# HGRN2 attention and a gelu MLP on one core: the decay's sigmoid through Tanh and GpSimd, and turned keys read in place by TensorE

## The chip, the cores and the metric

The kernel runs on one core of a Trainium2 chip. The core has a matrix engine (TensorE, PE in the profile, with its weight loads on a row of their own, PEld), VectorE (DVE), ScalarE (ACT), GpSimd (POOL) and a DMA issuer (SyncE, SP). The engines work side by side and wait for each other through semaphores. The metric is the device time of the launch in microseconds.

## The reference, cut to what matters

```python
# B, H, S, D = 4, 8, 768, 48; all float32
f = 1.0 / (1.0 + np.exp(-f_logit))
for t in range(S):
    state = f[:, :, t, :, None] * state + np.einsum('bhd,bhe->bhde', k[:, :, t], v[:, :, t])
    y[:, :, t] = np.einsum('bhd,bhde->bhe', q[:, :, t], state)
x = y.transpose(0, 2, 1, 3).reshape(3072, 384)
h = x @ w_in                                  # 384 -> 2048
g = h * (1.0 / (1.0 + np.exp(-1.702 * h)))
out = g @ w_out                               # 2048 -> 384
```

## The kernel before

The 3072 tokens are worked in 12 **units** of 256 tokens, n = 0 to 11, three for each of the four batches. Inside a unit the recurrence is not stepped token by token. The decays F = sigmoid(f_logit) are multiplied together in a tree of six levels (block lengths 1, 2, 4 to 32); at each level the keys and queries in X are scaled by the products (`promote`) and TensorE makes a product of keys and queries (`score`), so that a chunk of 64 tokens becomes a masked 64 by 64 matrix A. What a chunk hands on is a state of 48 by 48 for each head, made from turned keys (tokens on the partitions) and values. Each unit is held as two halves of 128 tokens, f = 1 in time order and f = 0 backwards, and as two heads (h) of four pairs (a).

After attention, a unit's 256 rows of y are brought into xT and go through the MLP: h = xT by `w_in` (line 785), g by one ScalarE instruction straight out of PSUM (line 789, `Gelu_apprx_sigmoid`), and the product with `w_out` (line 811 for the first three units, line 762 for the rest).

The lines that the change and the prediction touch:

- `begin_f`, line 358, through `turn`, line 326: brings the unit's f_logit into F, tokens along the free axis. Units 0 to 2 are turned by TensorE (line 344) and written out of PSUM by four ScalarE instructions (line 349), which apply the sigmoid on the way in units 0 and 1; unit 2 copies first and applies it in one instruction on the whole of F (line 355). Units 3 to 11 are turned by two VectorE transposes (line 332), and one ScalarE instruction over 128 x 1024 applies the sigmoid in place (line 337).
- `begin_gates`, line 377: six GpSimd multiplies (line 383) that make the tree of products `tot` from F. They are in one queue with whatever else GpSimd is given. Level 0 of `promote` reads F itself (line 473 in units 0 to 2, line 477 after).
- The turned keys `kn`. Units outside `CARRY` turn them on TensorE (line 532) and copy them out with ScalarE (line 533). The seven units in `CARRY`, n = 4 to 10, send them through memory instead: VectorE transposes blocks into z (line 540), four DMAs write them to a DRAM tile and one reads them back as kt, tokens on the partitions (line 554). In kt the four pairs of a column lie side by side: the innermost index is a. ScalarE copies kt to `kn`, where the columns of one pair are contiguous (line 555).
- Part "S", line 568: 64 matmuls (line 576), one for each pair, half, head and 64-token group, each with a 64 by 64 weight load from `kn`. They lie in turn on four quarters of the array (group g sets the rows, head h the columns). The states (lines 591 to 595, VectorE) are made from their result.

The order of the work on TensorE is written out by hand all through (`manual_schedule`): `merge` puts the matmuls of earlier units' MLP between the parts of a unit's attention. For the first four units the emission order holds on every engine (`fill_order`); from unit 4 on, the order on the other engines is a planner's. PSUM gives the products and turns four buffers in common (tag "mm"). kt and z take turns in three SBUF buffers (tag "sum"), `kn` and yT share one (tag "kn").

ScalarE's functions come from tables, and the sigmoid and the g of line 789 are in different ones: the compiler puts an ACT_TABLE_LOAD ahead of each change.

Of the kernel before, what the change touches and what calls it, by code (L numbers as in the profile page):

```python
# [9 lines left out]
F32 = mybir.dt.float32  # L10
I32 = mybir.dt.int32
U32 = mybir.dt.uint32
AF = mybir.ActivationFunctionType
ALU = mybir.AluOpType


def view(t, offset, dims):

    a = t[:]
    return bass.AP(a.tensor, a.offset + offset, [list(a.ap[0])] + [list(d) for d in dims])  # L20
# [3 lines left out]
def kernel(  # L24
# [33 lines left out]
    nc = tc.nc  # L58
# [3 lines left out]
    P = 128  # L62
# [6 lines left out]
    NP = H // 2  # L69
    HS = 64  # L70
# [6 lines left out]
    N_FILL = 3  # L77
    HALF = U // 2
    SLOT = NP * HALF
    NA = NP * U  # L80
    NALL = B * NU
    CARRY = range(N_FILL + 1, NALL - 1)
# [6 lines left out]
    mlp = ctx.enter_context(tc.tile_pool(name="mlp", bufs=2))  # L89
# [58 lines left out]
    F = const.tile([P, NA], F32, name="F")  # L148
# [21 lines left out]
    for r in range(NGR):  # L170
        ffs = range(r * FG, (r + 1) * FG)
        for ff in ffs[::2]:
            f = slice(ff * P, (ff + 2) * P)
# [65 lines left out]
    def load_raw(n, j, engines=(nc.sync,)):  # L239
        if n >= NALL:  # L240
            return
        b, s0 = n // NU, n % NU * U
        src = (f_logit, q, k)[j]
        first = s0 - (j == 1)

        def span(head, token, dims, d=0):
            return bass.AP(src.tensor, src.offset + ((b * H + head) * S + token) * D + d, dims)
        if n < N_FILL:
            for a in range(NP):
                engine = engines[a * len(engines) // NP]  # L250
                to = by_pair[j][32 * a:32 * (a + 1), :, :R * D]
                if first < 0 and a == 0:

                    for r, rows in ((1, 16), (17, 15)):
                        engine.dma_start(
                            out=to[r:r + rows], in_=span(0, r * R - 1, [[R * D, rows], [S * D, 2], [1, R * D]])
                        )
                    engine.dma_start(out=to[:1, :, D:], in_=span(0, 0, [[R * D, 1], [S * D, 2], [1, (R - 1) * D]]))
                else:
                    engine.dma_start(out=to, in_=span(2 * a, first, [[R * D, 32], [S * D, 2], [1, R * D]]))  # L260
            return
        for f in (1, 0):
            for r in range(4):
                lo = 32 * (r % 2)
                width = R4 * D - lo
                part = span(r // 2, first + (0 if f else HALF), [[R4 * D, 32], [2 * S * D, NP], [1, width]], lo)
                nc.sync.dma_start(out=by_half[32 * r:32 * (r + 1), j, f, :, :width], in_=part)
            if f and first < 0:
                for r in range(4):
                    lo = 32 * (r % 2)  # L270
                    nc.sync.dma_start(
                        out=by_half[32 * r:32 * r + 1, j, f, :, :D - lo],
                        in_=q[b - 1, r // 2::2, S - 1:S, lo:].rearrange("a t d -> t a d"),
                    )
# [31 lines left out]
    def attention(n):  # L306
# [8 lines left out]
        ORDER = (1, 0) if n % 2 == 0 else (0, 1)  # L315
        R_BASE, L_BASE = max(KR, QF) - 1, max(KF, QR) - 1
        t = {"tms": [F]}
        parts = []

        def part(kind):  # L320
            return lambda fn: parts.append((kind, fn))
# [4 lines left out]
        def turn(j, outs, fn=None):  # L326

            if n >= N_FILL:
                for f in (1, 0):
                    out = outs(f)  # L330
                    at, step = (0, 1) if f else (HALF - 1, -1)
                    nc.vector.transpose(  # L332
                        view(out, at, [[HALF, NP], [step, R4], [R4 * step, 32]]),
                        by_half[:, j, f].rearrange("p a (j d) -> p (a j) d", j=R4)[:, :, :32],
                    )
                if fn:
                    nc.scalar.activation(F, F, fn)
                return
            for j0 in range(0, R, 4):
                pt = ps.tile([P, 4, P], F32, tag="mm", name=f"t_{n}_{j}_{j0}", bufs=4)  # L340
                for jj in range(4):
                    for h in range(2):
                        x = (j0 + jj) * D
                        nc.tensor.matmul(  # L344
                            pt[h * HS:(h + 1) * HS, jj, :], lhsT=by_pair[j][:, h, x:x + HS], rhs=ident, start=True, stop=True
                        )
                for f in (1, 0):
                    at, step = (j0, 1) if f else (HALF - 1 - j0, -1)
                    nc.scalar.activation(
                        view(outs(f), at, [[HALF, NP], [R * step, 16], [step, 4]]),  # L350
                        pt.rearrange("p j (a f i) -> p f a i j", a=NP, f=2)[:, 1 - f],
                        fn if fn and n < N_FILL - 1 else AF.Copy,
                    )
            if fn and n == N_FILL - 1:
                nc.scalar.activation(F, F, fn)

        def begin_f():
            turn(0, lambda f: F[:, ORDER.index(f) * SLOT:(ORDER.index(f) + 1) * SLOT], AF.Sigmoid)
            if n >= N_FILL or (n == 1 and 0 == 0):
                load_raw(n + 1, 0)  # L360

        def begin():
            turn(1, lambda f: slot(query(n, f)))
            if n >= N_FILL or (n == 1 and 1 == 0):
                load_raw(n + 1, 1)
# [45 lines left out]
        def scores():  # L411
            t["sc"] = ps.tile([P, 2, NP, 2, HS], F32, tag="sc", name=f"sc_{n}_{next(serial)}")
            return t["sc"]
# [67 lines left out]
        def add():  # L481


            t["py"] = ps.tile([P, NG, NP, 2, HS], F32, tag="y", name=f"y_{n}")
            for a in range(NP):
                for f in (1, 0):
                    for h, g in TILES:
                        nc.tensor.matmul(  # L488
                            t["py"][columns(h, g), g, a, f, :],
                            lhsT=vts[n][g * HS:(g + 1) * HS, f, (2 * a + h) * D:(2 * a + h + 1) * D],  # L490
                            rhs=A[g * HS:(g + 1) * HS, h * NP + a, f, :],
                            start=(f == 1 and a == 0), stop=False, skip_group_check=True,
                        )
# [28 lines left out]
        def new_kn():  # L522
            t["kn"] = att.tile([P, NP, 2, P], F32, tag="kn", name=f"kn_{n}", bufs=1)
# [24 lines left out]
                )  # L548

        def fetch_k(f):  # L550
            if f == 0:
                new_kn()
            z = mlp.tile([P, P, NP], F32, tag="sum", name=f"kt_{n}_{f}", bufs=3)
            nc.sync.dma_start(out=z.rearrange("p d a -> p (d a)"), in_=k_toks[n % 2][f].rearrange("t i x -> t (i x)"))
            nc.scalar.copy(t["kn"][:, :, f, :], z.rearrange("p d a -> p a d"))

        if n not in CARRY:
            for a0 in (0, 2):
# [8 lines left out]
        @part("S")  # L567
        def _():
            add()
            pd = scores().rearrange("p h a s t -> p h (a s t)")  # L570
            for a in range(NP):
                for f in (1, 0):
                    for h in range(2):
                        for g in range(NG):
                            x = (a * 2 + f) * D
                            nc.tensor.matmul(  # L576
                                pd[h * HS:(h + 1) * HS, g, x:x + D],
                                lhsT=t["kn"][g * HS:(g + 1) * HS, a, f, h * HS:(h + 1) * HS],
                                rhs=vts[n][g * HS:(g + 1) * HS, f, (2 * a + h) * D:(2 * a + h + 1) * D],
                                start=True, stop=True,  # L580
                            )
            load_v(n + 1)
            st = att.tile([P, NC, NP, D], F32, tag="st", name=f"st_{n}", bufs=2)
            D64 = t["tms"][NL].rearrange("p (f a g) -> p f g a", f=2, a=NP)
            prev = t["ahead"] = last.get("st")
            t["before"] = [prev[:, NC - 1] if c == 0 and not first else st[:, c - 1] if c else None for c in range(NC)]
            for c in range(NC):
                g, f = CHUNK[c]
                d = pd[:, g, :NP * 2 * D].rearrange("p (a f e) -> p f a e", a=NP, f=2)[:, f]
                if t["before"][c] is None:  # L590
                    nc.vector.tensor_copy(st[:, c], d)
                    continue
                by = D64[:, ORDER.index(f), g].unsqueeze(2).broadcast_to((P, NP, D))
                nc.vector.tensor_tensor(st[:, c], t["before"][c], by, ALU.mult)  # L594
                nc.vector.tensor_tensor(st[:, c], st[:, c], d, ALU.add)
            last["st"] = st
# [418 lines left out]
```

## Time and profile before

Three runs took 628.22, 628.49 and 629.21 us, median 628.49; the profiled execution spans 627.9 us. The page gives a row to each engine; a busy time is a union, so overlapping matmuls are counted once.

| | us | count |
|---|---|---|
| span of the profiled execution | 627.9 | |
| DVE busy | 385.8 | 632 |
| ACT busy | 260.3 | 544 |
| of it: g, 128 x 256 and 128 x 257 | 72.1 | 192 |
| of it: table loads, 1.283 us each | 25.7 | 20 |
| of it: kt copied to kn, 128 x 512 | 15.9 | 14 |
| of it: sigmoid on the whole of F (lines 337, 355) | 10.6 | 10 |
| POOL busy | 39.9 | 91 |
| PE: the matmuls of part S, line 576 | 13.6 | 768 |

In the listing of instructions in order of time, a row gives the start, the length, the engine, the line, the operation with output and inputs, the number of instructions merged in the row, and in brackets how long the engine had stood idle before it and on whom it waited. "p*q" ahead of a matmul's shape is the rows and columns of the array that it uses.

### The profile page before, as it was taken

To read this page: it belongs to the slowest core of one execution; us is meant where nothing else is said; L and a number is where in the kernel's file an instruction comes from. 1 tells how busy PE (TensorE), PEld (TensorE's weight loads), DVE (VectorE), ACT (ScalarE), POOL (GpSimd) and SP (SyncE) were. 2 spreads that over 40 slices of the span, in tenths; PEclk is the share of its full clock that TensorE was granted. 3 is DMA by queue.
4 is the path that set the end of the run, shared out by engine and by line. 5 is a ranking of instruction groups with operands and counts; after the bars stand their busy time and mean duration, and the time that the engine had idled before them with its cause. 6 is when DMAs were issued, how large, how long until landed. Compare 5 with 4: busy or idle time off the path is not lost.

```text
span 627.9 us, 17094 instructions
## 1 busy us (share of the span) xinstructions
PE 602.8 (96%) x7314; PEld 517.5 (82%) x7314; DVE 385.8 (61%) x632; ACT 260.3 (41%) x544; POOL 39.9 (6%) x91
## 2 busy tenths in 40 slices
PE   7958999889999999999999999999999999999997
PEld 5647776757678688989989989989989889889896
DVE  1778976575876755677566577656658645521441
ACT  3436543533244534543544454354354353233220
POOL 3010030020001001001001001001001001000000
PEclk9898999989999999999999999999999999999999
DMA  7646675652034444444452342552161121001000
GB/s 171 183 126 165 170 161 158 148 139 76 2 92 99 122 100 105 105 94 110 122 135 60 76 109 73 142 123 68 45 160 33 44 59 27 27 1 27 26 1 25
DMA packets 83308, 58.20 MB, mean 93 GB/s; under 512 B 33633, under 2 KB 75265, under 8 KB 83233
## 3 DMA queue, kind: packets, MB, share of 16 engines
q1 hardware_dynamic: 82192, 55.55, 35.4%
q10 hardware_dynamic: 1041, 1.57, 1.0%
q8 instruction: 57, 0.93, 0.7%
q14 instruction: 18, 0.15, 0.1%
HBM read 43.98 MB, written 8.39 MB: 83 GB/s over the span
## 4 chain that ended last, share of the span: by engine, by line
PE 87%; DVE 6%; ACT 3%; DMA 2%; issue 1%; SPq 1%; ACTq 0%; DVEq 0%
PE h L785 38%; PE o_X L762 8%; PE o_Y L762 8%; PE o L811 8%; PE o_Z L762 7%; PE sc L392 6%; PE o_W L762 4%; PE t L344 3%; PE y L616 2%; PE sc L576 2%; PE y L488 1%; PE idle L108 1%; DVE a L221 1%; DMA xT<-yT 1%; ACT yT L627 1%
## 5 line engine op out<-in xcount | busy, mean ns | idle before, releaser
L785 PE MATMUL h<-xT,w_in 128*128 128x256 f32 (+1 forms) x1152 | 257.4, 381 | 2.4 <-ACT g L789 1.9
L785 PEld LDWEIGHTS h<-xT,w_in 128*128 128x128 f32 x1152 | 216.4, 190 | 34.2 <-ACT g L789 2.1
L789 ACT ACTIVATE g<-h 128x256 f32<-128x256 f32 (+1 forms) x192 | 72.0, 383 | 156.8 <-PE h L785 156.5
L477 DVE TENSOR_TENSOR X<-X,tot 128x1024 f32<-128x1024 f32 x45 | 55.1, 1224 | 62.6 <-PE sc L392 49.4
L448 ACT COPY Kc<-X 128x512 f32<-128x512 f32 x72 | 48.0, 666 | 83.4 <-DVE X L477 51.3
L811 PE MATMUL o<-w_out,g 128*128 128x384 f32 x192 | 67.5, 501 | 3.0 <-DVE w_out L222 3.0
L811 PEld LDWEIGHTS o<-w_out,g 128*128 128x128 f32 x192 | 36.2, 194 | 26.0 <-DVE w_out L222 3.6
L762 PE MATMUL o_X<-w_out,g 128*128 128x192 f32 x288 | 52.6, 331 | 0.0
L762 PE MATMUL o_Y<-T,S 128*128 128x192 f32 x288 | 51.9, 329 | 0.0
L441 DVE COPY_PREDICATED A<-masks,sc 128x256 f32<-128x256 uint32 (+1 forms) x108 | 50.9, 534 | 0.1
L762 PEld LDWEIGHTS o_Y<-T,S 128*128 128x128 f32 x288 | 46.9, 190 | 1.5 <-issue 0.7
L762 PEld LDWEIGHTS o_X<-w_out,g 128*128 128x128 f32 x288 | 46.7, 190 | 1.0
L383 POOL TENSOR_TENSOR tot<-F 128x512 f32<-128x512 f32 x12 | 12.5, 1039 | 478.2 <-DVE st L594 429.3
L392 PE MATMUL sc<-X,Kc 48*64 48x64 f32 x1440 | 31.1, 224 | 10.7 <-ACT Kc L448 9.6
L392 PEld LDWEIGHTS sc<-X,Kc 48*64 48x64 f32 x1440 | 26.4, 138 | 18.0 <-ACT Kc L448 11.4
L332 DVE STREAM_TRANSPOSE X<-raw 128x512 f32<-128x512 f32 x36 | 37.9, 1101 | 2.9 <-PE y L616 2.8
L700 DVE TENSOR_TENSOR g<-g,g 128x512 f32<-128x512 f32 x18 | 12.5, 692 | 40.4 <-ACT g L789 40.4
L627 ACT COPY yT<-y 48x256 f32<-48x256 f32 x92 | 33.7, 366 | 7.8 <-PE y L616 5.3
L473 DVE TENSOR_TENSOR X<-X,tot 128x512 f32<-128x512 f32 x30 | 20.3, 688 | 13.1 <-PE sc L392 11.0
L383 POOL TENSOR_TENSOR tot<-tot 128x256 f32<-128x256 f32 (+4 forms) x60 | 24.6, 410 | 4.7
L762 PE MATMUL o_W<-T,g 128*128 128x192 f32 x144 | 24.9, 326 | 0.0
L762 PE MATMUL o_Z<-w_out,g 128*128 128x192 f32 x144 | 24.9, 326 | 0.0
(92 smaller groups left out, 629.1 us busy)
## 6 DMA issues: line engine op xcount, KB each, us to landing
bits<-in_moe_w_out_dram SPq DMA_DIRECT2D x8, 768.0 KB, 5.0
raw<-in_f_logit_dram SPq DMA_DIRECT2D x48, 96.0 KB, 2.3
raw<-in_k_dram SPq DMA_DIRECT2D x48, 96.0 KB, 2.3
raw<-in_q_dram SPq DMA_DIRECT2D x44, 96.0 KB, 2.3
bits<-in_moe_w_in_dram SPq DMA_DIRECT2D x7, 576.0 KB, 6.2
k_tok<-z SPq DMA_DIRECT2D x56, 64.0 KB, 1.8
kt<-k_tok SPq DMA_DIRECT2D x14, 256.0 KB, 2.8
out_dram<-osb SPq DMA_DIRECT2D x18, 192.0 KB, 1.8
```

Of the source, the lines that this page charges most:

```text
L332: nc.vector.transpose(view(out, at, [[HALF, NP], [step, R4], [R4 * step, 32]]), by_half[:, j, f].rearrange("p a (j d) -> p (a j) d", j=R4) ...
L383: nc.gpsimd.tensor_tensor(tn, t2[:, :, 0], t2[:, :, 1], ALU.mult)
L392: nc.tensor.matmul(t["sc"][g * HS:(g + 1) * HS, h, a, s, :], lhsT=t["Kc", l][rows(h), x:x + HS], rhs=rhs(h, a, g), start=True, stop=True,)
L441: nc.vector.copy_predicated(out=view(A, at, dims), mask=mask.bitcast(U32), data=got)
L448: nc.scalar.copy(c.rearrange("p (n two m) -> p n two m", two=2, m=m), view(X, KF * SLOT, [[2 * m, SLOT // (2 * m)], [(KR - KF) * SLOT + m, ...
L473: nc.vector.tensor_tensor(x, x, y, ALU.mult)
L477: nc.vector.tensor_tensor(x, x, y, ALU.mult)
L627: copy(view(yT[rows(h)], at, [[U, NP], [step, HS]]), py[columns(h, g), g, :, f, :])
L762: nc.tensor.matmul(t[bank], lhsT=lhs(f), rhs=rhs(f), start=(new and f == 0), stop=(f == HF - 1), skip_group_check=True,)
L785: nc.tensor.matmul(ph, lhsT=w_in[:, c, ff * P:(ff + 1) * P], rhs=xTs[n][:, c, :], start=(c == 0), stop=(c == NK - 1))
L789: nc.scalar.activation(g[ff // FG][:, ff % FG, :], ph, AF.Gelu_apprx_sigmoid)
L811: nc.tensor.matmul(t["po"], lhsT=g[ff // FG][:, ff % FG, tt * P:(tt + 1) * P], rhs=w_out[:, ff, :], start=(ff == ffs[0]), stop=(ff == ffs[ ...
```

## The change

The sigmoid is computed as 0.5 tanh(x/2) + 0.5 in all units but the first. Tanh is to come from the table that also holds g's function, so that ScalarE needn't change tables for each unit; GpSimd does the halving and the addition in place on F (`half_up`), ahead of the tree of products. In unit 2 the function is now applied by the four instructions that bring F out of PSUM. In the `CARRY` units ScalarE no longer copies kt to `kn`: TensorE's weight loads read a pair's column straight from kt, with a step of four elements (16 bytes) from one channel to the next.

```diff
@@ turn @@
                 if fn:
-                    nc.scalar.activation(F, F, fn)
+                    fn()
                 return
...
                     nc.scalar.activation(
                         view(outs(f), at, [[HALF, NP], [R * step, 16], [step, 4]]),
                         pt.rearrange("p j (a f i) -> p f a i j", a=NP, f=2)[:, 1 - f],
-                        fn if fn and n < N_FILL - 1 else AF.Copy,
+                        (AF.Tanh if n else AF.Sigmoid) if fn else AF.Copy, scale=0.5 if fn and n else 1.0,
                     )
-            if fn and n == N_FILL - 1:
-                nc.scalar.activation(F, F, fn)
+            if fn and n:
+                half_up()
+
+        def half_up():
+            nc.gpsimd.tensor_scalar(F, F, 0.5, 0.5, op0=ALU.mult, op1=ALU.add)
+
+        def sigmoid():
+            nc.scalar.activation(F, F, AF.Tanh, scale=0.5)
+            half_up()
 
         def begin_f():
-            turn(0, lambda f: F[:, ORDER.index(f) * SLOT:(ORDER.index(f) + 1) * SLOT], AF.Sigmoid)
+            turn(0, lambda f: F[:, ORDER.index(f) * SLOT:(ORDER.index(f) + 1) * SLOT], sigmoid)
...
         def fetch_k(f):
-            if f == 0:
-                new_kn()
-            z = mlp.tile([P, P, NP], F32, tag="sum", name=f"kt_{n}_{f}", bufs=3)
+            z = t["kt", f] = mlp.tile([P, P, NP], F32, tag="sum", name=f"kt_{n}_{f}", bufs=3)
             nc.sync.dma_start(out=z.rearrange("p d a -> p (d a)"), in_=k_toks[n % 2][f].rearrange("t i x -> t (i x)"))
-            nc.scalar.copy(t["kn"][:, :, f, :], z.rearrange("p d a -> p a d"))
+
+        def turned_k(p, a, f, d):
+            return t["kt", f][p, d, a] if n in CARRY else t["kn"][p, a, f, d]
...
                                 pd[h * HS:(h + 1) * HS, g, x:x + D],
-                                lhsT=t["kn"][g * HS:(g + 1) * HS, a, f, h * HS:(h + 1) * HS],
+                                lhsT=turned_k(slice(g * HS, (g + 1) * HS), a, f, slice(h * HS, (h + 1) * HS)),
                                 rhs=vts[n][g * HS:(g + 1) * HS, f, (2 * a + h) * D:(2 * a + h + 1) * D],
```

## The prediction

> **What bounds the kernel now.** I read the page's engine rows first, then the busy times by stretch, then TensorE's waits, then the timeline where those waits are. The rows of the stretches give start:end and length, then busy time and number of instructions of each engine.
>
> ```profile
> PE 602.8 (96%) x7314; PEld 517.5 (82%) x7314; DVE 385.8 (61%) x632; ACT 260.3 (41%) x544; POOL 39.9 (6%) x91
> ```
> ```profile
> 45.00:113.00 68.00, 63.04 (x812) 46.91 (x813) 54.81 (x93) 32.10 (x64) 4.75 (x6) 0.95 0.66 160
> 113.00:195.00 82.00, 76.46 (x774) 55.89 (x773) 55.90 (x80) 33.83 (x62) 4.19 (x6) 0.98 0.37 93
> ...
> 332.30:378.10 45.80, 45.80 (x597) 42.05 (x597) 29.71 (x47) 20.97 (x43) 2.81 (x6) 1.00 0.35 84
> ```
> The reader is to see two regimes. From 195 us on TensorE has no free time: a CARRY unit lasts 45.8 us and PE is busy for 45.8. ScalarE is at 21 of 45.8 there, so making it faster buys nothing by itself. Idle TensorE time lies in the first 195 us: 10.6 us before 45, 5.0 in 45 to 113, 5.5 in 113 to 195. Only there, or in the time of a TensorE instruction itself, can this change move the end.
>
> Of TensorE's waits on ScalarE that the change could touch, one is large:
> ```profile
> 115.53 1.28 ACT L337 ACT_TABLE_LOAD   x1
> ...
> 116.82 1.06 ACT L337 ACTIVATE F<-F 128x1024 f32<-128x1024 f32 x1
> 117.78 0.89 ACT L217 ACTIVATE a<-bits 128x768 f32<-128x768 f32 x1
> 118.69 1.28 ACT L789 ACT_TABLE_LOAD   x1
> 119.99 0.38 ACT L789 ACTIVATE g<-h 128x256 f32<-128x256 f32 x1
> 120.42 3.75 PEld L785 LDWEIGHTS h<-xT,w_in 128*128 128x128 f32 x18 [2.11 <-ACT g L789]
> 120.42 4.15 PE L785 MATMUL h<-xT,w_in 128*128 128x256 f32 x18 [1.87 <-ACT g L789]
> ```
> Two table loads stand between two g's, and PE is out of PSUM buffers for 1.87 us. Within 241 to 515 us the waits on ScalarE are these two, each once:
> ```profile
> PE sc L576 <- ACT kn L555: 0.5, 1, 0.5
> ...
> PEld o_Y L762 <- ACT p L736: 0.3, 1, 0.3
> ```
>
> [...]
> ```profile
> 129.09 1.04 POOL L383 TENSOR_TENSOR tot<-F 128x512 f32<-128x512 f32 x1 [45.46 <-DVE st L594]
> 129.23 1.72 DVE L221 SCALAR_TENSOR_TENSOR a<-bits,a 128x768 f32<-128x768 uint32 x1
> ```
> That VectorE instruction takes 0.96 elsewhere; it ended 0.8 us after GpSimd's. [...]that tanh is in g's table is the change's own statement. [...]Here 128 columns take 190 ns and 64 take 135: 0.86 ns a column[...].
>
> **Table loads.** There are 20. The one at the start stays, and one change to g's table; 18 go, 18 x 1.283 = 23.1 us of ScalarE. Worth on the path: at unit 3 the row of waits above. After the change Tanh starts at 115.53, ends at 116.6, L217 at 117.5, the g of 119.99 is done by 117.9. PE's last turn ended at 118.55, so it goes on at once. What hangs on it then: VectorE's L595 stood 4.6 us for PE's L576, its conversions come after, and PE's wait for w_out at 132.28 (2.96 us) waits for those, so the whole chain moves: **-1.9**. At unit 4 (179 to 183 us) PE doesn't wait around the loads, and from 195 it never does: 0, hidden by TensorE's own work. The 0.26 us (0.3 above) before o_Y, on a ScalarE queue made late by loads and copies, I count as gone: **-0.3**.
>
> **Unit 2's separate sigmoid** (L355, 1.06 us at 52.78) goes; ScalarE reaches the Kc copy at 56.27 earlier, and PE's 1.28 us wait at 56.93 could shrink by 1.06. But VectorE works without a gap from 49.7 to 81 but for about 0.36 us, and PE waits for it again at 76.6 to 78.8 and, through Kc, at 82.5. So 0.36 at most is kept.
>
> **half_up**, 11 times 128 x 1024 on GpSimd. No row shows it. [...]Upper: the two-input rows, 1039 ns at 512 and 693 at 256, carried on to 1024: 1.73. I take 1.2. F is then ready 1.06 + 1.2 = 2.26 us after the transposes instead of 1.28 + 1.06 = 2.34: no later. Behind it in GpSimd's queue is only the same unit's tot tree, which starts some 40 us later in steady state (it waits for st L594). So the new wait costs nothing[...]. At unit 1 (28 us) VectorE has gaps: **+0.1**. At unit 2 (52.8 us) VectorE is gapless with two-input work and can lose 0 to 1.2: half of it, 0.6, less about half of the 0.36 above: **+0.4**. From unit 3 on VectorE idles (118.7: 2.82 us) or has slack (30 of 45.8).
>
> **The copy kt to kn** goes: 14 x 1.133 = 15.9 us of ScalarE, hidden behind TensorE save the one wait of 0.46 (0.5 above) in unit 4: **-0.5**. The S matmuls now wait for the DMA: issued at 325.38 and 2.8 us to landing, 328.2, against their start at 333.1. kt keeps its buffer until S; its next taker writes 27 us later. 0.
>
> **The weight loads with a step**, 7 x 64. This is the disputed cost.
> ```profile
> L448 ACT COPY Kc<-X 128x512 f32<-128x512 f32 x72 | 48.0, 666 | 83.4 <-DVE X L477 51.3 <-DVE X L332 15.8 <-DVE X L473 10.4
> ...
> L555 ACT COPY kn<-kt 128x512 f32<-128x512 f32 x14 | 15.9, 1133 | 0.0
> ...
> L337 ACT ACTIVATE F<-F 128x1024 f32<-128x1024 f32 x9 | 9.5, 1060 | 0.1
> ```
> ```profile
> 333.11 1.03 PEld L576 LDWEIGHTS sc<-vt,kn 64*64 64x64 f32 x64
> ```
> ```profile
> 566.02 0.45 PEld L634 LDWEIGHTS y_last<-q_end,st 48*48 48x48 f32 x16
> ```
> ScalarE read this very kt with this very step: 1133 ns for 512 elements. Without it the ordinary Kc copies take 0.62 and F's 1024 elements 1060, that is 0.86 ns an element and 180 ns fixed. So the step costs (1133 - 180) / 512 = 1.86 ns an element, 2.16 times. Is the S stage bound by reading weights? 64 loads end within 1.03 us, each 0.135: (1.03 - 0.135) / 63 = 14.2 ns from one to the next[...]. The 16 y_last loads are the test: their matmuls have one column, they use two quarters, [...](0.45 - 0.122) / 15 = 21.9 measured. [...]So if a column with a step takes twice as long, S takes twice as long: 64 x (27.6 - 14.2) = 0.86 us a unit, on TensorE, which has no slack: 7 x 0.86 = **+6.0**. Lower bound 0[...]. Upper bound: [...]4 x, 7 x 2.8 = +20. I take twice[...].
>
> Sum: -1.9 - 0.3 + 0.1 + 0.4 - 0.5 + 6.0 = +3.8; 628.5 + 3.8 = **632.3 us**.
>
> **The rivals.** (a) The step is free for weight loads: the sum without 6.0 is -2.2, 626.3, faster. For it: [...]nothing in the trace shows it slowed; against it: [...]the 2.16. (b) The step costs half as much more (the alternating Kc copy at 134.93 takes 0.85 instead of 0.62, 1.5 times an element): [...]+3.0, so 629.3, hardly to be told from now. (c) [...]it costs three to four times: +13 to +20, 640 to 646. For it only that two head quarters read the same partitions[...]. That tanh is not in g's table would add 1.9 to each of these, and I hold it for unlikely.
>
> **How the numbers follow.** Forecast 0.50, (a) 0.34, (b) 0.10, (c) 0.06. The range goes from (a) with VectorE losing nothing at unit 2 (626.3 - 0.6, 625.7) to the forecast with ScalarE's 2.16 and half_up at its upper end (64 x 15.5 x 7 = 6.9 for 6.0, and 0.5 more: 633.7). It leaves out (c) and little else. Faster by over 0.2% (below 627.2): (a), less a little, 0.33. Slower (above 629.8): forecast, (c) and a fifth of (b), 0.58. Between: 0.09.
>
> **What would show it.** Part S's 64 weight loads at about 1.9 us instead of 1.03, a single one near 190 instead of 135 ns, and a CARRY unit at 46.7 instead of 45.8: the forecast. 1.03 and 45.8: rival (a). Two table loads in all. No wait on g near 118 us, and the stretch 113 to 195 shorter by 1.9. [...]A VectorE instruction stretched near 53 us. The forecast is wrong if S keeps its length, or if the planner's new order from unit 4 on makes TensorE wait where it doesn't now.

## The result, and the profile after

| | median us | lowest to highest | runs |
|---|---|---|---|
| before | 628.85 | 628.22 to 629.34 | 4 |
| changed | 632.44 | 631.07 to 633.68 | 4 |

The ratio is 1.0057, interval 1.0034 to 1.0081: slower by 3.6 us (2.1 to 5.1). The profiled execution of the changed kernel is its fastest, with a span of 629.3.

The row of engines of the page after:

```profile
PE 607.2 (96%) x7314; PEld 523.5 (83%) x7314; DVE 388.6 (62%) x632; ACT 223.8 (36%) x511; POOL 53.0 (8%) x102
```

The change did what it set out to do for ScalarE: 36.5 us less busy time (260.3 to 223.8), at 13.1 us more of GpSimd. TensorE, with the same 7314 matmuls, is busy for 4.4 us more, its weight loads for 6.0.

**Table loads.** The listing by form of the changed kernel; after the bar come busy us and mean ns:

```profile
L112 ACT ACT_TABLE_LOAD x1 | 1.3, 1283 | 0.7 <-PEq L1007 0.7
L797 ACT ACT_TABLE_LOAD x1 | 1.3, 1283 | 0.0
```

Two are left of 20, so Tanh does come from the table of g. Where the kernel before had the row of loads and the wait on g at unit 3, the changed kernel's listing in order of time now shows:

```profile
112.74 0.38 ACT L797 ACTIVATE g<-h 128x256 f32<-128x256 f32 x1 [0.91 <-PE h L793]
113.02 1.05 ACT L362 ACTIVATE F<-F 128x1024 f32<-128x1024 f32 x1
...
113.97 0.92 ACT L217 ACTIVATE a<-bits 128x768 f32<-128x768 f32 x1
114.16 1.04 POOL L359 TENSOR_SCALAR F<-F 128x1024 f32<-128x1024 f32 x1 [32.95 <-ACT F L362]
...
114.78 0.38 ACT L797 ACTIVATE g<-h 128x256 f32<-128x256 f32 x1
```

Tanh and the weight conversion follow each other, and g comes right behind; no row of TensorE there has a wait on g.

**Part S.** One line's instructions in the changed kernel: name, count, then shortest/median/longest ns, first and last start. The `kt` rows are the CARRY units, the `kn` rows the others:

```profile
L584 PEld LDWEIGHTS sc<-vt,kt x448: 188/213/215, 236.0 to 518.7; 64*64 64x64 f32 x150
L584 PE MATMUL sc<-vt,kt x448: 260/280/282, 236.1 to 518.7; 64*64 64x48 f32 x150
L584 PEld LDWEIGHTS sc<-vt,kn x320: 129/135/135, 30.8 to 560.3; 64*64 64x64 f32 x160
```

A load with the step takes 213 ns, one without it 135, in the same kernel. The chain of work that ended last, first of the changed kernel (unit 5) and then of the kernel before (unit 7), start and length:

```profile
282.03 1.04 PE y L496 x64
283.07 1.90 PE sc L584 x64
284.97 2.80 PE o_X L770 x16
```
```profile
378.13 1.04 PE y L488 x64
379.17 0.92 PE sc L576 x64
380.09 2.80 PE o_X L762 x16
```

The neighbours keep their lengths; S alone grew, by 0.98, and it stands on the chain with no gap on either side.

**Unit by unit.** I take the start of each unit's `y<-A,vt` matmuls, which run right before part S, as its mark. From unit 1's mark to unit 2's, and from unit 7's to unit 8's (the rows of stretches, the changed kernel first; the three last numbers are the clock that TensorE was granted, as a share of full speed, the busy share of the DMA engines, and GB/s):

```profile
67.45:119.98 52.53, 51.66 (x587) 39.18 (x586) 39.25 (x65) 22.19 (x48) 5.79 (x7) 1.00 0.68 161
375.58:422.40 46.82, 46.82 (x594) 43.07 (x593) 29.88 (x47) 16.80 (x39) 3.87 (x7) 1.00 0.44 112
```
```profile
69.92:124.51 54.59, 51.92 (x588) 39.22 (x587) 39.05 (x65) 24.72 (x50) 4.75 (x6) 1.00 0.68 161
378.06:423.89 45.83, 45.83 (x593) 42.09 (x592) 29.61 (x47) 21.02 (x43) 2.81 (x6) 1.00 0.47 114
```

The first stretch lost 2.06 us with TensorE's work unchanged (51.9 to 51.7): a wait went. The second gained 0.99 with TensorE busy all through in both: its own work grew. The experiments below are read by the same marks (each row is one profiled execution):

| us from mark to mark, units | 0 to 1 | 1 to 2 | 4 to 5 | 5 to 6 | 7 to 8 | 0 to 11 |
|---|---|---|---|---|---|---|
| before | 38.03 | 54.59 | 46.52 | 46.09 | 45.83 | 525.25 |
| changed | 37.48 | 52.53 | 46.81 | 46.82 | 46.82 | 528.56 |
| e1, Tanh without the step | 37.58 | 52.54 | 46.53 | 45.83 | 45.83 | 522.51 |
| e2, step without Tanh | 37.46 | 54.60 | 46.82 | 47.04 | 46.82 | 530.87 |
| e3, changed, step of 4 bytes | 37.43 | 52.52 | 45.84 | 45.84 | 45.83 | 521.66 |
| e4, changed, step of 8 bytes | 37.77 | 52.55 | 45.87 | 45.86 | 45.86 | 522.22 |
| e5, e3 with units 0 to 2 as before | 37.50 | 52.48 | 45.84 | 45.83 | 45.84 | 521.69 |
| e6, Tanh from unit 4, with copy | 38.26 | 54.61 | 46.52 | 45.84 | 45.84 | 525.20 |
| e7, Tanh from unit 3, with copy | 38.12 | 52.49 | 46.53 | 45.83 | 45.84 | 522.98 |
| e8, e3 without half_up in units 1 and 2 | 37.61 | 52.52 | 45.83 | 45.83 | 45.84 | 521.80 |
| e9, the same kernel as e3 | 38.61 | 52.52 | 45.83 | 45.84 | 45.84 | 525.17 |
| e10, the same kernel as e5 | 37.19 | 52.45 | 45.84 | 45.83 | 45.84 | 521.32 |

The marks leave out what comes before unit 0's. There single executions differ for reasons outside the change: the profiled one of the changed kernel reached unit 0's mark 1.9 us earlier than that of the kernel before (29.97 against 31.89), and two groups of four matmuls at line 108, one ahead of the first scores and one right after them, took 1.6 us each there instead of 2.6 and 2.5. Part of this goes with the granted clock: up to unit 0's mark it was 1.00 in the changed kernel and 0.95 in the kernel before, whose second group (16.73 to 19.26) had 0.59. The first group had 1.00 in both, and why it took longer is not known. From unit 0's mark to the end of the span the changed kernel is longer by 599.3 - 596.0 = 3.3, close to the measured 3.6; the spans alone would say 1.4.

Two executions of one kernel differ inside the marks as well. e9 is e3 over again, and its profiled execution, at a mean clock of 0.984 over the span (e3: 0.992), lost 1.2 us from unit 0 to 1 and 2.3 us from unit 2 to 3. From unit 1 to 2, and from unit 3 on, kernels that are alike there agree within 0.1 us, and the readings of single terms below, but for half_up's, rest on these stretches.

### The profile page after: what moved, and what is told of

Read it like the earlier page. It is cut to its first block, busy times and chain, and to the rows that moved or that the text cites. A ratio compares the mean times of both kernels' runs of the same rounds, so it can differ in the third digit from the quotient of the medians.

```text
span 629.3 us, 17074 instructions
## 1 busy us (share of the span) xinstructions
PE 607.2 (96%) x7314; PEld 523.5 (83%) x7314; DVE 388.6 (62%) x632; ACT 223.8 (36%) x511; POOL 53.0 (8%) x102
## 4 chain that ended last, share of the span: by engine, by line
PE 85%; DVE 7%; DMA 3%; ACT 2%; issue 1%; SPq 1%; DVEq 0%; ACTq 0%
PE h L793 37%; PE o_X L770 8%; PE o_Y L770 8%; PE o L819 8%; PE o_Z L770 7%; PE sc L400 6%; PE o_W L770 4%; PE sc L584 2%; PE y L624 2%; PE t L344 2%; PE y L496 1%; DVE X L481 1%; ACT yT L635 1%; DMA bits<-in_moe_w_in_dram 1%; DVE a L221 1%
## 5 line engine op out<-in xcount | busy, mean ns | idle before, releaser
L770 PE MATMUL o_Y<-T,S 128*128 128x192 f32 x288 | 51.7, 329 | 0.0
L770 PE MATMUL o_Z<-T,g 128*128 128x192 f32 x144 | 24.9, 326 | 0.0
```

The costliest lines, as they stand in the source:

```text
L770: nc.tensor.matmul(t[bank], lhsT=lhs(f), rhs=rhs(f), start=(new and f == 0), stop=(f == HF - 1), skip_group_check=True,)
```

## The experiments

Theory: the step doubles the weight loads of S on an engine without slack (+6 to 7), the table loads were worth one wait (-2), the rest is small. Rivals: the time is lost elsewhere, in the new wait on the transfer or in GpSimd's half_up; or any step hurts, and not only one of 16 bytes. e1 to e4 and the kernel before ran on one chip (before: 628.66, 39 runs).

### e1: Tanh without the step

The changed kernel with the copy to `kn` kept:

```diff
+            nc.scalar.copy(t["kn"][:, :, f, :], z.rearrange("p d a -> p a d"))
...
-                                lhsT=turned_k(slice(g * HS, (g + 1) * HS), a, f, slice(h * HS, (h + 1) * HS)),
+                                lhsT=t["kn"][g * HS:(g + 1) * HS, a, f, h * HS:(h + 1) * HS],
```

> The changed kernel with the copy from kt to kn kept: only the Tanh half of the change. If the step of the weight loads is what costs (my theory), this is faster than before: -2.1 at unit 3, +0.6 at unit 2, -0.3 at one wait, so about 627.0 us, weight loads of part S at 135 ns and a CARRY unit at 45.8 us. If the Tanh half itself costs ([...]another order from the planner), it stays at 631 to 633 us.

Measured 627.28 us (14 runs), ratio 0.9986 (0.9974 to 0.9997). The CARRY unit is back at 45.83. Tanh and half_up by themselves make the kernel slightly faster; the loss isn't theirs. (The recorded ratios need not be those of the two medians.)

### e2: the step without Tanh

The kernel before, with no copy and `lhsT` read from kt:

```diff
-            nc.scalar.copy(t["kn"][:, :, f, :], z.rearrange("p d a -> p a d"))
+        def turned_k(p, a, f, d):
+            return t["kt", f][p, d, a] if n in CARRY else t["kn"][p, a, f, d]
```

> The kernel before with its sigmoid and all its table loads, but the weight loads of part S reading kt with a step of four elements. Step theory: 7 x 0.98 - 0.5 = +6.4, about 635.2 us, with the weight loads of S at 213 ns and S at 1.9 us. If the Tanh half costs and not the step: 628.3 us.

Measured 635.74 us (4 runs), ratio 1.0124 (1.0109 to 1.0139). Its line of part S is that of the changed kernel:

```profile
L576 PEld LDWEIGHTS sc<-vt,kt x448: 188/213/216, 238.3 to 521.3; 64*64 64x64 f32 x150
```

The CARRY unit is 46.82. So the slowdown is in this half of the change alone. From mark to mark it gained 5.6 us; the medians say 7.1, with only four runs of this kernel.

### e3: the changed kernel without a step

If the step is the cause, it must go away when the same bytes lie otherwise in kt, still without a copy. The blocks are written with the pair a outside, and four transfers of runs of 128 bytes bring each kt in, where one brought it before:

```diff
-                z.rearrange("p b d a -> p a b d"),
+                z.rearrange("p b a d -> p a b d"),
...
-            z = t["kt", f] = mlp.tile([P, P, NP], F32, tag="sum", name=f"kt_{n}_{f}", bufs=3)
-            nc.sync.dma_start(out=z.rearrange("p d a -> p (d a)"), in_=k_toks[n % 2][f].rearrange("t i x -> t (i x)"))
+            z = t["kt", f] = mlp.tile([P, NP, P], F32, tag="sum", name=f"kt_{n}_{f}", bufs=3)
+            for a in range(NP):
+                nc.sync.dma_start(
+                    out=z[:, a].rearrange("p (i d) -> p i d", d=32), in_=k_toks[n % 2][f][:, :, a * 32:(a + 1) * 32]
+                )
...
-            return t["kt", f][p, d, a] if n in CARRY else t["kn"][p, a, f, d]
+            return t["kt", f][p, a, d] if n in CARRY else t["kn"][p, a, f, d]
```

> The changed kernel with kt laid out by pairs, so that TensorE reads it in place without a step and without a copy; z is laid out by pairs too, and four DMAs with runs of 128 bytes bring kt in, where there was one. Step theory: the weight loads of S go back to 135 ns, S to 1.03 us, a CARRY unit to 45.8, and the time to about 626.3 us. If reading weights from the tile that a DMA has filled, or holding that tile until S, is what costs: S stays at 1.9 us and the time at 632. If the smaller DMAs land too late, TensorE waits at S for a DMA.

Measured 626.27 us (12 runs), ratio 0.9966 (0.9951 to 0.9980).

```profile
L587 PEld LDWEIGHTS sc<-vt,kt x448: 133/135/135, 236.6 to 512.5; 64*64 64x64 f32 x150
```

The matmuls, their data, the missing copy and the wait on the transfer are those of the changed kernel; the place of the bytes, the transfers and VectorE's transposes into z differ. (The transposes, which no longer write with a step, take 0.70 us each instead of 1.11; but it is S that shrinks, from 2.01 us to 1.03.) The CARRY units 4 to 9 fall to 45.84 and unit 10 by as much (42.51 to 41.53), and from unit 4's mark to unit 11's it is 316.54 against 323.38: the step cost **6.84 us**, with the copy's wait absent on both sides. That the S matmuls wait for a transfer instead of ScalarE costs nothing: unit 4 to 5 is even shorter than with the copy (45.84, against 46.53 in e1).

### e4: a step of 8 bytes

Two pairs side by side instead of four. VectorE's transposes are split in two for it, and two transfers bring kt in:

```diff
-            z = mlp.tile([P, nb, NP, 32], F32, tag="sum", name=f"z_{n}_{f}", bufs=3)
+            z = mlp.tile([P, nb, 2, 32, 2], F32, tag="sum", name=f"z_{n}_{f}", bufs=3)
...
-            return t["kt", f][p, a, d] if n in CARRY else t["kn"][p, a, f, d]
+            return t["kt", f][p, a // 2, d, a % 2] if n in CARRY else t["kn"][p, a, f, d]
```

> As e3, but with two pairs side by side in kt: a step of two elements, 8 bytes[...]; two DMAs with runs of 256 bytes, and VectorE turns each half in two instructions. [...]as e3, loads of S at 135 ns, about 626.3 us. If any step costs: loads of S at about 213 ns and 632 us; if the cost grows with the step, something between, about 629.

Measured 626.59 us (20 runs), ratio 0.9973 (0.9961 to 0.9986).

```profile
L588 PEld LDWEIGHTS sc<-vt,kt x448: 134/135/137, 237.9 to 513.9; 64*64 64x64 f32 x150
L588 PE MATMUL sc<-vt,kt x448: 206/220/222, 237.9 to 514.0; 64*64 64x48 f32 x150
```

So it isn't the step as such. With 8 bytes S runs nearly as without a step (its 64 matmuls take 1.13 us against 1.10 in e3, and from unit 4's mark to unit 11's it is 316.72 against 316.54), with 16 at about half the rate (2.08 us in e2). Why the loads slow down between these two steps is not shown. Steps between 8 and 16 bytes, or beyond 16, were not tried.

### e6 and e7: from which unit Tanh pays

Both are the kernel before with the copy kept; e7 uses Tanh and half_up from unit 3 on, e6 from unit 4. Their only difference is unit 3, whose sigmoid stands in the row of table loads. (With e5, on a second chip; before: 629.29, 34 runs.)

```diff
         def sigmoid():
-            nc.scalar.activation(F, F, AF.Tanh, scale=0.5)
-            half_up()
+            if n > N_FILL:
+                nc.scalar.activation(F, F, AF.Tanh, scale=0.5)
+                half_up()
+            else:
+                nc.scalar.activation(F, F, AF.Sigmoid)
```

> The kernel before with the copy to kn kept, Tanh and half_up only from unit 4 on: 16 of the 20 table loads go, 20.5 us of ScalarE, but the two around unit 3's sigmoid stay. If the gain lies in the one wait at unit 3 and ScalarE's load is hidden elsewhere: -0.3, about 628.4 us, with TensorE's wait of 1.9 us on g still there. If the table loads cost everywhere (1.3 us each on the path, or a share of it): -2 or more, 626 us or less.

> As e6 but Tanh and half_up from unit 3 on: two loads fewer than e6. If the one wait is the gain: 1.9 to 2.1 us faster than e6, about 626.4 us, TensorE's wait on g near 118 us gone and the way from unit 2's to unit 3's product of A and values 52.5 us instead of 54.6. If the gain is spread over the loads: 0.2 us faster than e6.

e6: 629.44 us (22 runs), ratio 1.0001 (0.9987 to 1.0016): no gain to be told. The 0.3 that was expected is below what this interval tells. e7: 626.50 us (10 runs), ratio 0.9954 (0.9938 to 0.9971). In e6 sixteen table loads are gone and four are left; the listing in order of time has two of these at unit 3, with the old wait behind them:

```profile
114.19 1.28 ACT L366 ACT_TABLE_LOAD   x1
...
115.49 1.06 ACT L366 ACTIVATE F<-F 128x1024 f32<-128x1024 f32 x1
...
117.35 1.28 ACT L800 ACT_TABLE_LOAD   x1
...
119.08 1.13 PE L796 MATMUL h<-xT,w_in 128*128 128x256 f32 x4 [1.86 <-ACT g L800]
```

Unit 1's mark to unit 2's is 54.61 in e6 and 52.49 in e7; nothing else in the table of marks tells them apart by more than 0.14. Two table loads are worth 2.1 us and the other sixteen 0.25, the latter between the marks of units 5 and 6 (46.09 to 45.84).

### e5, e8, e9, e10: what half_up costs in units 1 and 2

e5 is e3 with units 0 to 2 as in the kernel before:

```diff
-                        (AF.Tanh if n else AF.Sigmoid) if fn else AF.Copy, scale=0.5 if fn and n else 1.0,
+                        AF.Sigmoid if fn and n < N_FILL - 1 else AF.Copy,
                     )
-            if fn and n:
-                half_up()
+            if fn and n == N_FILL - 1:
+                nc.scalar.activation(F, F, AF.Sigmoid)
```

> e3 with units 0 to 2 as in the kernel before: Sigmoid as they come out of PSUM (unit 2 in one instruction on F), no half_up; Tanh and half_up from unit 3 on. If half_up in unit 2 costs about 0.6 us [...]while VectorE is the bound, this is that much faster than e3, about 625.7 us, VectorE's two-instruction promote near 51 us back from 2.13 to 1.28. If the separate sigmoid that returns (1.06 us of ScalarE) is worth more[...], it is slower than e3, about 626.9.

624.88 us (9 runs), ratio 0.9942 (0.9921 to 0.9964): the lowest median, and more below e3 than half_up was to cost. To see whether that holds, e3 and e5 were run again on a third chip (before: 629.44, 11 runs), beside e8, which is e3 less these two lines and so leaves tanh(x/2) as the decay of units 1 and 2:

```diff
-            if fn and n:
-                half_up()
```

> e3 with half_up left out in units 1 and 2, so those two units' decays are tanh(x/2) and their results not the reference's; all else as e3. If [...]the early half_up costs, this is 0.5 to 1.5 us faster than e3 and as fast as e5 or up to 1 us faster, since the separate sigmoid of unit 2 is gone as well. If e5's lead over e3 was the spread of two chips, it is within 0.3 us of e3.

> e3 on the same chip as e8 and e10, to compare them without a change of chip: 626.0 to 626.5 us.

> e5 on the same chip as e3: 0.6 to 1.4 us faster than it if half_up in units 1 and 2 costs; equal if e5's lead was the spread of two chips.

| | median us | runs | ratio |
|---|---|---|---|
| e8, no half_up in units 1 and 2 | 626.23 | 6 | 0.9949 (0.9931 to 0.9968) |
| e9, the same kernel as e3 | 626.25 | 7 | 0.9943 (0.9923 to 0.9964) |
| e10, the same kernel as e5 | 625.89 | 6 | 0.9945 (0.9925 to 0.9965) |

The three can't be told apart, so e5's lead over e3 was not confirmed. The traces don't settle the term either. VectorE does lose time: in the changed kernel's listing its pair of multiplies took 2.13 us beside unit 2's half_up, against 1.28 before,

```profile
50.32 1.44 POOL L359 TENSOR_SCALAR F<-F 128x1024 f32<-128x1024 f32 x1 [10.48 <-ACT F L349]
```
```profile
50.77 2.13 DVE L481 TENSOR_TENSOR X<-X,tot 128x512 f32<-128x512 f32 x2
```

but from unit 0's mark to unit 1's, where this lies, kernels with half_up take 37.43 to 38.61 and kernels with the old front 37.19 to 38.26. The same front varies there by 1.1 or more, and the term to be found is 0.5. Before unit 0's mark, beside unit 1's half_up, TensorE stood still among its score matmuls for 0.42 us in e1 and 1.56 in e4, with nothing that the trace shows to wait for, but not in the changed kernel, where half_up took the same 1.51. What half_up costs in these two units stays open: e8 and e9 have medians 0.02 us apart, with over 1 us of uncertainty in each.

e3 and e5 are the best versions: about 0.3 to 0.6% below the kernel before, each in two comparisons. e7, which keeps the copy, has a ratio in the same range; only the marks put it behind them, by 1.3 us.

## Why the prediction was right

Forecast 632.3, measured 632.44. Term by term, from the differences between kernels:

| term | predicted | measured | from |
|---|---|---|---|
| weight loads with the step | +6.0 | +6.84 | changed less e3, unit 4's mark to unit 11's |
| unit 3's wait on g | -1.9 | -2.1 | e7 less e6, unit 1's mark to unit 2's |
| copy to kn, unit 4 | -0.5 | -0.7 | e3 less e1, unit 4's mark to unit 5's |
| wait before o_Y | -0.3 | -0.25 | e6 less before, unit 5's mark to unit 6's |
| half_up, units 1 and 2 | +0.5 | not resolved | e3, e5, e8 to e10 |

The mechanism was right: the step on TensorE, the one wait at unit 3 and the small waits are where the runs put them. That the change in time is right to 0.2 us is in part luck. The four measured terms sum to +3.8; the same four were predicted at +3.3, and half_up's +0.5, which the runs don't show, filled the gap. Within the four the step was 0.8 too small, and the waits took 0.35 of it back.

**The step.** The doubling held. It was an estimate: the kernel before has no weight load with a step, and the factor was ScalarE's (1133 ns for 512 elements with the step, 2.16 times an element). That S is bound by reading columns was an estimate as well. A weight load of 128 columns takes 190 ns (`w_in`, `w_out`) and one of 64 takes 135, so 0.86 ns a column; in S, over four quarters of the array, 64 columns make 13.8 ns, against a spacing of 14.2, and in `y_last`, over two, 48 make 20.6, against 21.9. But the 128-column loads of `tkn` take 141 ns, so the trace doesn't settle it. The change stretched the loads' spacing from 14.2 to 28.5 ns: 64 loads end within 2.01 us, each 0.213, so (2.01 - 0.213) / 63. That is twice; what was mis-sized is the sum over it. The prediction put the spacing at 27.6; its text doesn't derive it, but twice 13.8 is 27.6. That gave 13.4 ns for each of 64 loads, 0.86; in fact the whole 14.2 doubled, 14.3 x 63 = 0.90, and the last load's own length grew by 0.08: 0.98 a unit, 6.9 in seven. ScalarE's own factor of 2.16, kept for the end of the range, gives 6.9 as well, but the trace shows a factor of two, so that is no confirmation of it. Of the single loads, forecast at 190 ns, only the first four of a unit, one for each quarter, are that (188 to 190), and the other 60 take 210 to 215. Rival (a), a free step, is nearly what e4 shows for 8 bytes; for 16 it fell. Rival (c), three to four times, fell with it, and (b), one and a half times, too.

**Unit 3.** It went as worked out: Tanh done 1.05 after its start, the conversion, then g, and TensorE goes on. The gain exceeds the removed wait's 1.87 by 0.2; what the rest is stays open.

**The copy.** The row of waits said 0.46. It counts TensorE's idle time from the end of the matmuls before; from start to start, S began 1.58 us after the mark in e1 and 0.93 in e3, so the wait cost 0.65, nearly all of the 0.7. To size a wait on a saturated engine, the distance between starts is the better measure.

**half_up.** The 1.2 us was an estimate, as were the +0.1 and +0.4, which had one pair of rows behind them (a VectorE instruction of 1.72 us for 0.96 beside GpSimd's 1.04). The mean is as taken, 1.205 us, and from unit 3 on no cost shows (e7 has before's length in every unit from 6 on). But the eleven are not alike:

```profile
L359 POOL TENSOR_SCALAR F<-F x11: 1044/1085/1719, 25.9 to 479.5; 128x1024 f32<-128x1024 f32 x11
```

Eight of the eleven take 1.04 to 1.10; the other three, in units 1, 2 and 4, take 1.44 to 1.72. Each of these three started 0.53 to 0.82 us ahead of the end of a VectorE multiply with two inputs, and is 0.40 to 0.67 longer than the shortest; in units 2 and 4 VectorE's next such multiply is longer as well (1.52 us for 0.68, 1.79 for 0.96). The stretched VectorE instruction that was forecast near 53 us was there, at 50.8; that it reached the end of the kernel was not shown.

## What to carry to other kernels

When TensorE has no free time, what its own instructions take longer lengthens the kernel, and a busy ScalarE counts only in the waits that end last: here 36.5 us off ScalarE bought 3.0 us, and 14.3 ns more from each of 448 weight loads to the next took back 6.8. Before a copy that only straightens a layout is removed, see who reads the layout then, and with what step: in these runs the 64 float32 weight loads and matmuls of S took 1.10 us at 4 bytes, 1.13 at 8 and 2.08 at 16. If the producer or the transfer can lay the data out straight, as in e3, both gains are had.

## What the runs showed of the hardware beyond this

- The matmuls of S are longer in the profile with the step in their loads: 280 ns against 218 with the same moving data, 62 ns more, where the load itself grew by 78. The profile models the ends of matmuls, so this is less sure than the spacing of the loads.
- A step of 8 bytes costs next to nothing: 135 ns a load as without a step, 1.13 us for the matmuls of S against 1.10, and CARRY units of 45.86 us against 45.84. I had only the two ends in mind, free or not.
- VectorE's transposes of 128x512 into z take 1.11 us where they write with a step of 16 bytes (the kernel before and the changed one) and 0.70 where they write without one (e3).
- Four transfers of 64 KB with runs of 128 bytes, in place of one of 256 KB for each kt, cost the kernel nothing: e3's CARRY units (45.84 us, units 5 to 6) equal those of e1 (45.83), which has the one transfer.
- What precedes unit 0's mark varies by 2.1 us among profiled executions of kernels that are alike up to there (30.23 in e2, 32.34 in e7), and it goes with the mean granted clock: of the kernel before, the changed one and e1 to e7, the five with 0.991 or more over the span reach the mark at 29.97 to 31.44, the four with 0.989 at 31.48 to 32.34.
- Whole runs follow the clock in the same way. On the first chip the 39 runs of the kernel before took 627.8 us on average at a mean clock of 0.995 (8 runs), 629.1 at 0.989 (13) and 630.6 at 0.986 (5). Of the 50 runs of e1 to e4 only one had 0.995, and all four kernels come out 1.0 to 1.5 us slower against the kernel before by their medians than by the marks; that the clock is the whole reason is not shown. Differences below about half a microsecond are better read from mark to mark, in stretches with the same clock, than from medians of ten runs.
